# Experts' token rows: loaded from ScalarE's queue when the buffer is free, always as 112 partitions, and place 1 transposed two turns later

## The chip, the cores and the metric

The kernel runs on one core of one Trainium2 chip. The metric is the device time of one execution in microseconds, median of several runs.

## The reference

Four batches of 768 tokens go through a gated linear recurrence of eight heads (48 columns each), then through a mixture of eight experts of which each token takes one, then through a dense layer of 2048 hidden columns. All is float32.

```
state = alpha_t * state + k_t v_t        # per batch and head; y_t = q_t state
x = y as [3072, 384]
idx = argmax(x @ w_gate); g = softmax(x @ w_gate)[idx]
x = g * (relu(x @ w1[idx]) @ w2[idx])    # w1: 384 x 1024, w2: 1024 x 384
h = x @ w_in                             # 384 x 2048, comes as float64
out = (max(h, 0) + alpha2 * min(h, 0)) @ w_out
```

## The kernel before

The first 218 us or so are the recurrence (by chunks, as products) and the routing: each token's row goes by indirect DMA (`scatter`, L514, GpSimd's queue) to its expert's part of the table `xs` in DRAM, which has room for 448 rows (`CAP`) per expert. The six scatters of the last batch are still under way when the experts start.

The experts run in the order of their number of tokens, by places 0 to 7. `CAPS` gives the tokens that a place computes: 448, 448, 440, 424, 416, 400, 392, 384. A place has eight turns `f`; in a turn `expert_L1` makes 128 hidden columns of the first layer (9 products into `ph`), ScalarE writes their relu `hh`, VectorE the rest `hl`, and `expert_L2` adds the turn of two turns ago to the three sums `acc` (9 products). Each operand is the sum of two parts (`xh` and `xl`, `w1h` and `w1l`, `hh` and `hl`), so each product is three.

The rows of the next place are read by `expert_x` into the one buffer `xg`, in one DMA on SP's queue: as `CAPS[e] // 4` partitions of 4 rows, so 112, 110, 106, 104, 100, 98 and 96 partitions for the places 1 to 7. It is issued before the loop for place 1, and in turn 1 of the place before for the others. In turns 3, 4 and 5 `expert_xT` transposes 128 columns each into `pt` (TensorE), and `expert_xsplit` makes `xh` (ScalarE) and `xl` (VectorE) of them. `row_i` and `off_i` are tables with the place's first row in `xs` and its first place in the output; an engine that issues a DMA from there first reads them into a register (`value_load`). `expert_meta` copies the rows' gate weights and token numbers to `meta`.

Beside this, jobs on weights are handed out by turns (`job`, `one_job`). A `split` job loads a quarter of an expert's weights into `r1` and `r2` (SP's queue, three jobs ahead), copies them as `w1h` and `w2h` on ScalarE and subtracts on VectorE (`w1l`) and GpSimd (`w2l`). An `f64` job brings a piece of `w_in` or `w_out` from float64 to float32 by its bits: `fabs` on ScalarE (L166), four operations on VectorE (L169 to L173), and a store from SP's queue (L174). Place 0 has four f64 and four split jobs, places 1, 3 and 5 six and four, places 2 and 4 five and four, places 6 and 7 four split jobs alone.

The order of each engine's instructions is the order in which the code is written, and what a DMA has to wait for, the engine that issues it waits for. When the experts start, GpSimd clears the output table `yT` (L1201), which lies where the last rows were and so waits for the last scatter.

Of the kernel before, what the change touches and what calls it, by code (L numbers as in the profile page):

```python
# [20 lines left out]
P = 128  # L21
# [11 lines left out]
#: tokens that a place in the order of experts takes: the first expert, then the others, the fullest first  # L33
# [8 lines left out]
#: the upper word of 2**-126 as a float64, its bits read as a float32  # L42
# [4 lines left out]
class Kernel:  # L47
# [7 lines left out]
    # ------------------------------------------------------------ constants  # L55
# [11 lines left out]
    def constants(self, cp, ap):  # L67
# [11 lines left out]
        # per pair of heads: the 96 real columns of a padded 128, then the gate weights' rows  # L79
# [52 lines left out]
    # ------------------------------------------------------------ expert weights  # L132
    def w_src(self, e):
        """by place: the first expert, the others in their order, then the halves of the second layer"""
        if e == 0:
            return self.w1[0], self.w2[0]
        if e < E:
            if self.wreg[0] != e:
                self.wreg = e, self.nc.sync.value_load(self.perm_i[0:1, e:e + 1], min_val=0, max_val=E - 1)
            r = self.wreg[1]  # L140
            return (w[ds(r, 1)].rearrange("o a b -> (o a) b") for w in (self.w1, self.w2))
        h = e - E
        return self.w_in32[:, F * h:F * (h + 1)], self.w_out32[F * h:F * (h + 1), :]

    # w_in and w_out come as float64: here each is brought to float32, by its bits
# [14 lines left out]
    def f64_piece(self, n, raw, pool):  # L160
# [11 lines left out]
        # what float32 has no exponent for goes to zero  # L172
# [3 lines left out]
    # jobs on the weights, by their turns; what each reads is loaded some jobs ahead  # L176
# [68 lines left out]
    # ------------------------------------------------------------ attention  # L245
# [16 lines left out]
    def warm(self, n, cols=BLK):  # L262
        """products of no use while the first loads are under way: the array's clock comes up by them"""
        if n:
            ps = self.psg.tile([P, cols], F32, name="psw", tag="psG")
        for _ in range(n):
            self.nc.tensor.matmul(ps, self.wm, self.wm[:, 0:1].to_broadcast([P, cols]), start=True, stop=True)
# [51 lines left out]
    def attn_alpha(self, u, half, ps=None):  # L319
# [4 lines left out]
        # a decay outside the range is the recurrence's; here it only has to stay finite  # L324
        nc.vector.tensor_scalar(self.seq(self.sl[u % 2]["E"][:, 0:S], half), ps, ALO, AHI, ALU.max, ALU.min)

    def attn_scan(self, u, half=None):
        """decays from each step to its chunk's end and from the chunk's start, of all chunks or of half of them"""
# [101 lines left out]
    def attn_back(self, u, half):  # L430
# [12 lines left out]
        # the last logits are waited for, elsewhere the rows are  # L443
# [9 lines left out]
    # ------------------------------------------------------------ routing  # L453
    def route1(self, b, r, rp):
        """one-hot expert of a batch's tokens"""
# [18 lines left out]
    def route_gate(self, r, rp):  # L474
        """gate weight goes with the row"""
# [10 lines left out]
    def route2(self, b, rp):  # L486
        """slot of each token"""
# [24 lines left out]
    def scatter(self, dst, idx, src, n, group):  # L512
        """rows of src to rows of dst; those of a group go to rows that differ, so they need no order"""
# [13 lines left out]
    def totals(self, rp):  # L527
        """the experts' order, where each one's tokens start in it, and what lies beyond the capacities"""
# [42 lines left out]
    def attention(self, cp, rp, pp):  # L571
        nc, tc = self.nc, self.tc
        with ExitStack() as st:
            ap = st.enter_context(tc.tile_pool(name="attn", bufs=1))
            # what the unit before the last is done with makes room for the first expert's tokens
# [14 lines left out]
            # the first unit by halves, so that its products start early  # L590
# [126 lines left out]
    # ------------------------------------------------------------ the first expert's tokens  # L717
    # Those of the batches before the last come from xs. Those of the last batch are put in their columns by
    # products with one-hot rows, so that the first expert need not wait for their way through DRAM.
# [32 lines left out]
    def first_ranks(self, rp):  # L752
        """rank of the last batch's tokens in the first expert; far below 0 for those of others"""
# [19 lines left out]
    def ranks(self, ps, oh, before):  # L773
        """tokens of the same expert before each: in its tile, in the batch's tiles before it, before the batch"""
# [8 lines left out]
    # ------------------------------------------------------------ the experts  # L783
    def expert_rows(self, e):
        """rows of a place's expert"""
        r = 0 if e == 0 else self.nc.sync.value_load(self.row_i[0:1, e:e + 1], min_val=0, max_val=NSLOT - CAP)
        return self.xs[ds(r, CAPS[e]), :] if e else self.xs[0:CAPS[0], :]

    def expert_x(self, e):
        nc = self.nc  # L790
        rows = self.expert_rows(e)
        xg = self.op.tile([CAPS[e] // 4, 4, DM], F32, name="xg", tag="xg", bufs=1)
        nc.sync.dma_start(xg, rows[:, 0:DM].rearrange("(j p) w -> p j w", j=4))
        return xg, rows

    def expert_meta(self, e, rows):
        """gate weights and tokens go to their place in the experts' order"""
# [4 lines left out]
    def expert_xT(self, xg, x, m):  # L802
        nc = self.nc
        q = xg.shape[0]
        ps = self.pt.tile([P, 4 * q], F32, name="pt", tag="pt")
        for j in range(4):
            nc.tensor.transpose(ps[:, q * j:q * (j + 1)], xg[:, j, P * m:P * (m + 1)], self.ident[:q, :q])
# [10 lines left out]
    def mm3(self, ps, pairs, start, stop):  # L818
        """sum of products of operands that are each the sum of two parts"""
# [12 lines left out]
    def first_L1(self, w, f, x, n, first):  # L832
        """products of a turn of the first layer; of the first two turns, those with the last rows of x come last"""
# [41 lines left out]
    def experts(self):  # L875
# [15 lines left out]
        xgn, rows = self.expert_x(1)  # L891
        for e in range(E):
            for f in range(NF):
# [3 lines left out]
                if f == 1 and 0 < e < E - 1:  # L897
                    xgn, rows = self.expert_x(e + 1)
                if f >= 3 and f < 3 + NM and e + 1 < E:
                    if f == 3:  # L900
                        xn = self.expert_xset(e + 1)
                    self.expert_xT(xgn, xn, f - 3)
                self.job(self.gp, (e, f))
                if f == 5 and e == 0:
                    self.expert_meta(0, self.expert_rows(0))
                if f == 7 and e + 1 < E:
                    self.expert_meta(e + 1, rows)
            if e + 1 < E:
                x = xn
        # the last two turns by parts of the output, which the second layer takes up one after another  # L910
# [7 lines left out]
    # ------------------------------------------------------------ the second layer  # L918
# [39 lines left out]
    def ffn(self):  # L958
# [21 lines left out]
        # the last three turns, so that the tiles end one after another  # L980
# [3 lines left out]
    # ------------------------------------------------------------ what the fast path does not cover  # L984
# [9 lines left out]
    def recurrence(self, st):  # L994
        """For a decay outside [ALO, AHI]: the recurrence step by step, then the routing again."""
# [77 lines left out]
    def overflow(self):  # L1073
        """Tile after tile of tokens go through every expert and keep their own's; those beyond a capacity are put out."""
        nc, tc = self.nc, self.tc
        NF = F // P
        with tc.tile_pool(name="ovt", bufs=1) as sb:
            t = lambda n, s, d=F32: sb.tile(s, d, name=n, tag=n)
            # a token is put out where it is beyond its expert's capacity, or the fast path covers none
# [14 lines left out]
            # rows that no token was put in  # L1094
# [73 lines left out]
    # ------------------------------------------------------------ all of it  # L1168
    def run(self):
        nc, tc = self.nc, self.tc  # L1170
        with ExitStack() as st, tc.manual_schedule():
# [11 lines left out]
            # on the other side: the last rows are on their way to DRAM when the experts start  # L1183
# [57 lines left out]
```

## Time and profile before

| | |
|---|---|
| time, median of 3 runs | 906.2 us (901.11 to 907.78) |
| profiled execution, its span | 908.3 us; no other time of it is given |
| TensorE busy | 844.6 us, 93% |
| VectorE, ScalarE, GpSimd busy | 496.8, 304.9, 322.2 us |
| TensorE waiting for `xg`, 200 to 470 us | 33.3 us in 6 waits |
| moved by DMA | 90.53 MB, mean 100 GB/s |

Busy shares are means over stages that differ: the DMA engines are busy until about 470 us and nearly idle after that, while TensorE is busy to the end. So the rows to read are those of the experts' stage, about 218 to 490 us. The granted clock is TensorE's, as a share of 2.4 GHz; its other level is 0.5.

### The profile page before, as it was taken

What the parts mean: (1) busy time and instruction counts of PE and PEld (TensorE: products, weight loads), DVE (VectorE), ACT (ScalarE), POOL (GpSimd) and SP (SyncE); (2) the same over time, 40 slices, a digit from 0 to 9 for tenths busy, and PEclk for the clock granted to TensorE, in tenths of its full rate; (3) what the DMA queues carried; (4) which work ended last, traced back from release to release, by engine and by line L of the source; (5) the groups of instructions that cost most, each with busy time, mean ns of one, the idle gap of its engine ahead of it and who ended that gap; (6) DMA issues with size and microseconds to landing.
All of it is one profiled execution on the core that took longest, in us unless ns stands there. A gap on an engine that the chain in (4) does not pass through costs nothing. (4 is left out here: it accounts for less than half of the span.)

```text
span 908.3 us, 14260 instructions
## 1 busy us (share of the span) xinstructions
PE 844.6 (93%) x5330; PEld 745.1 (82%) x5330; DVE 496.8 (55%) x892; ACT 304.9 (34%) x596; POOL 322.2 (35%) x323
## 2 busy tenths in 40 slices
PE   7999999889899397798999999999999999999993
PEld 4777777659799297798899899999999999899993
DVE  8579797946978185677434543343343343343331
ACT  3455555542444153354344322122122112212111
POOL 6232525553622021122232724324334334325232
PEclk9799999978899698999999999999999999999997
DMA  9899898432685457659644000000000000000001
GB/s 145 169 255 196 177 159 175 93 102 85 200 246 165 144 139 229 211 171 265 192 118 106 19 1 18 18 1 25 11 1 33 3 1 35 1 1 35 1 1 39
DMA packets 153155, 90.53 MB, mean 100 GB/s; under 512 B 112716, under 2 KB 145780, under 8 KB 153076
## 3 DMA queue, kind: packets, MB, share of 16 engines
q1 hardware_dynamic: 148963, 74.45, 35.1%
q0 software_dynamic: 4112, 15.08, 4.6%
q8 instruction: 44, 0.72, 0.4%
q14 instruction: 36, 0.29, 0.1%
HBM read 68.14 MB, written 21.40 MB: 99 GB/s over the span
## 5 line engine op out<-in xcount | busy, mean ns | idle before, releaser
L941 POOL TENSOR_TENSOR gl<-g,gh 128x512 fp32r<-128x512 f32 x94 | 122.0, 1298 | 232.0 <-ACT gh L940 231.8
L938 DVE TENSOR_SCALAR g<-ph,al 128x512 f32<-128x512 f32 (+1 forms) x97 | 72.2, 744 | 225.0 <-PE ph L825 225.0
L823 PE MATMUL ph<-xh,w1h 128*128 128x512 f32 (+7 forms) x480 | 184.5, 384 | 0.0
L825 PE MATMUL ph<-xh,w1l 128*128 128x512 f32 (+7 forms) x480 | 184.5, 384 | 0.0
L824 PE MATMUL ph<-xl,w1h 128*128 128x512 f32 (+7 forms) x480 | 184.3, 384 | 0.0
L940 ACT CAST gh<-g 128x512 fp32r<-128x512 f32 (+1 forms) x97 | 59.7, 616 | 315.7 <-DVE g L939 297.8
L238 POOL TENSOR_TENSOR w2l<-r,w2h 128x768 fp32r<-128x768 f32 x38 | 74.9, 1973 | 206.2 <-ACT w2h L237 206.2
L825 PE MATMUL acc<-w2h,gl 128*128 128x384 f32 x384 | 130.0, 338 | 0.0
L823 PE MATMUL acc<-w2h,gh 128*128 128x384 f32 x384 | 129.3, 337 | 0.0
L824 PE MATMUL acc<-w2l,gh 128*128 128x384 f32 x384 | 129.0, 336 | 0.0
L825 PEld LDWEIGHTS ph<-xh,w1l 128*128 128x128 f32 x480 | 92.2, 192 | 12.8
L824 PEld LDWEIGHTS ph<-xl,w1h 128*128 128x128 f32 x480 | 92.3, 192 | 10.8 <-DVE xl L925 0.4
L823 PEld LDWEIGHTS ph<-xh,w1h 128*128 128x128 f32 x480 | 92.2, 192 | 9.9
L823 PEld LDWEIGHTS acc<-w2h,gh 128*128 128x128 f32 x384 | 72.2, 188 | 4.2
L824 PEld LDWEIGHTS acc<-w2l,gh 128*128 128x128 f32 x384 | 72.1, 188 | 4.1
L825 PEld LDWEIGHTS acc<-w2h,gl 128*128 128x128 f32 x384 | 72.0, 188 | 0.9 <-POOL gl L941 0.6
L823 PE MATMUL acc<-hh,w2h 128*128 128x448 f32 (+6 forms) x192 | 68.6, 358 | 0.0
L939 DVE SCALAR_TENSOR_TENSOR g<-ph,g 128x512 f32<-128x512 f32 (+1 forms) x97 | 66.5, 686 | 3.3
L824 PE MATMUL acc<-hl,w2h 128*128 128x448 f32 (+6 forms) x192 | 68.3, 356 | 0.0
L825 PE MATMUL acc<-hh,w2l 128*128 128x448 f32 (+6 forms) x192 | 68.1, 354 | 0.0
L380 POOL TENSOR_SCALAR_AFFINE_SELECT A<-A 128x384 f32<-128x384 f32 x64 | 38.5, 624 | 57.4 <-ACT A L379 57.4
L858 ACT ACTIVATE hh<-ph 128x448 fp32r<-128x448 f32 (+6 forms) x64 | 33.3, 520 | 76.0 <-PE ph L825 76.0
(178 smaller groups left out, 1230.9 us busy)
## 6 DMA issues: line engine op xcount, KB each, us to landing
r<-in_moe_w_dram SPq DMA_DIRECT2D x64, 384.0 KB
r<-in_moe_w_in_dram SPq DMA_DIRECT2D x16, 384.0 KB
r<-in_moe_w_out_dram SPq DMA_DIRECT2D x16, 384.0 KB
xs<-z POOLq DMA_DIRECT2D x7, 776.0 KB
k<-in_k_dram SPq DMA_DIRECT2D x32, 144.0 KB
q<-in_q_dram SPq DMA_DIRECT2D x32, 144.0 KB
v<-in_v_dram SPq DMA_DIRECT2D x32, 144.0 KB
a<-in_alpha_dram SPq DMA_DIRECT2D x30, 144.0 KB
```

Source lines behind the costliest of these rows:

```text
L238: (nc.gpsimd if r is r2 and not self.fast else nc.vector).tensor_tensor(l, r, h.bitcast(F32), ALU.subtract)
L380: nc.gpsimd.affine_select(out=a, in_=a, pattern=[[0, 3], [1, P]], compare_op=ALU.is_ge, fill=0.0, base=0, channel_multiplier=-1)
L823: mm(ps, ah, bh, start=start and i == 0, stop=False)
L824: mm(ps, ah, bl, start=False, stop=False)
L825: mm(ps, al, bh, start=False, stop=stop and i == n - 1)
L858: nc.scalar.activation(hh, ph, AF.Relu)
L938: nc.vector.tensor_scalar(g[:, cs], ph[:, cs], 0.0, self.al2[:, f:f + 1], ALU.min, ALU.mult)
L939: nc.vector.scalar_tensor_tensor(g[:, cs], ph[:, cs], 0.0, g[:, cs], ALU.max, ALU.add)
L940: nc.scalar.copy(gh[:, cs], g[:, cs])
L941: lo.tensor_tensor(gl[:, cs], g[:, cs], gh[:, cs].bitcast(F32), ALU.subtract)
```

## The change

Three things change in the experts' stage. `expert_x` reads 448 rows whatever the place computes, as 112 partitions of 4 rows, and `expert_xT` transposes three groups of 112 columns and one of what is left of `CAPS[e]`. The DMA and the register load for it are on ScalarE's queue, not SP's; for places 2 to 7 they come right behind the third transpose of the place before, which frees the buffer. The transposes stand in turns 4 to 6, and for place 1 (during place 0) in turns 5 to 7. `expert_meta` now reads its own row number on SP. The rest of the diff takes out comments.

```diff
-    def expert_rows(self, e):
-        r = 0 if e == 0 else self.nc.sync.value_load(self.row_i[0:1, e:e + 1], min_val=0, max_val=NSLOT - CAP)
-        return self.xs[ds(r, CAPS[e]), :] if e else self.xs[0:CAPS[0], :]
+    def expert_rows(self, e, n, eng):
+        r = 0 if e == 0 else eng.value_load(self.row_i[0:1, e:e + 1], min_val=0, max_val=NSLOT - CAP)
+        return self.xs[ds(r, n), :] if e else self.xs[0:n, :]
     def expert_x(self, e):
-        nc = self.nc
-        rows = self.expert_rows(e)
-        xg = self.op.tile([CAPS[e] // 4, 4, DM], F32, name="xg", tag="xg", bufs=1)
-        nc.sync.dma_start(xg, rows[:, 0:DM].rearrange("(j p) w -> p j w", j=4))
-        return xg, rows
-    def expert_meta(self, e, rows):
+        if e >= E:
+            return None
+        eng = self.nc.scalar
+        xg = self.op.tile([CAP // 4, 4, DM], F32, name="xg", tag="xg", bufs=1)
+        eng.dma_start(xg, self.expert_rows(e, CAP, eng)[:, 0:DM].rearrange("(j p) w -> p j w", j=4))
+        return xg
+    def expert_meta(self, e):
+        rows = self.expert_rows(e, CAPS[e], self.nc.sync)
...
-    def expert_xT(self, xg, x, m):
+    def expert_xT(self, e, xg, x, m):
         nc = self.nc
-        q = xg.shape[0]
-        ps = self.pt.tile([P, 4 * q], F32, name="pt", tag="pt")
+        n, q = CAPS[e], CAP // 4
+        ps = self.pt.tile([P, n], F32, name="pt", tag="pt")
         for j in range(4):
-            nc.tensor.transpose(ps[:, q * j:q * (j + 1)], xg[:, j, P * m:P * (m + 1)], self.ident[:q, :q])
+            k = min(q, n - q * j)
+            nc.tensor.transpose(ps[:, q * j:q * j + k], xg[:k, j, P * m:P * (m + 1)], self.ident[:k, :k])
...
-        xgn, rows = self.expert_x(1)
+        xg = self.expert_x(1)
         for e in range(E):
             for f in range(NF):
...
-                if f == 1 and 0 < e < E - 1:
-                    xgn, rows = self.expert_x(e + 1)
-                if f >= 3 and f < 3 + NM and e + 1 < E:
-                    if f == 3:
+                m = f - (5 if e == 0 else 4)
+                if 0 <= m < NM and e + 1 < E:
+                    if m == 0:
                         xn = self.expert_xset(e + 1)
-                    self.expert_xT(xgn, xn, f - 3)
+                    self.expert_xT(e + 1, xg, xn, m)
+                    if m == NM - 1:
+                        xg = self.expert_x(e + 2)
                 self.job(self.gp, (e, f))
                 if f == 5 and e == 0:
-                    self.expert_meta(0, self.expert_rows(0))
+                    self.expert_meta(0)
                 if f == 7 and e + 1 < E:
-                    self.expert_meta(e + 1, rows)
+                    self.expert_meta(e + 1)
```

The first place to see is ScalarE at the start of place 0. `px` are the first expert's columns, `r` the pieces of weights. Before:

```order
L812 CAST xh_83<-px 128x448 x3
L858 ACTIVATE hh<-ph 128x448
L166 ACTIVATE fabs<-r_2316 128x384
L858 ACTIVATE hh<-ph 128x448
L166 ACTIVATE fabs<-r_2473 128x384
```

Now, the same stretch:

```order
L817 CAST xh_83<-px 128x448 x3
L786 TENSOR_LOAD row_i
L786 ISA x2
L796 ISA
L796 DMA xg<-xs 112x4x384
L863 ACTIVATE hh<-ph 128x448
L166 ACTIVATE fabs<-r_2316 128x384
L863 ACTIVATE hh<-ph 128x448
```

The load of place 1's rows, with its wait for the last scatter, stands ahead of the first relu on ScalarE.

The second place is ScalarE later in place 0, from the third f64 job on. Before:

```order
L166 ACTIVATE fabs<-r_2592 128x384
L858 ACTIVATE hh<-ph 128x448
L812 CAST xh_2780<-pt 128x448
L237 CAST w1h_2821<-r_2847 128x3x256
L237 CAST w2h_2823<-r_2849 128x768
L858 ACTIVATE hh<-ph 128x448
L812 CAST xh_2780<-pt 128x448
```

Now, the same stretch, up to the first copy of transposed rows:

```order
L166 ACTIVATE fabs<-r_2592 128x384
L863 ACTIVATE hh<-ph 128x448
L237 CAST w1h_2821<-r_2847 128x3x256
L237 CAST w2h_2823<-r_2849 128x768
L863 ACTIVATE hh<-ph 128x448
L237 CAST w1h_2821<-r_2898 128x3x256
L237 CAST w2h_2823<-r_2900 128x768
L863 ACTIVATE hh<-ph 128x448
L817 CAST xh_2780<-pt 128x448
```

Place 1's first copy from `pt` stands two relus further down.

The third place is ScalarE in place 1, around the last transposes of place 2's rows. Before:

```order
L812 CAST xh_83<-pt 128x440
L237 CAST w1h_73<-r_3256 128x3x256
L237 CAST w2h_75<-r_3258 128x768
L858 ACTIVATE hh<-ph 128x448
L166 ACTIVATE fabs<-r_3298 128x384
```

Now, from the same copy on, which stands a turn later:

```order
L817 CAST xh_83<-pt 128x440
L786 TENSOR_LOAD row_i
L786 ISA x2
L796 ISA
L796 DMA xg<-xs 112x4x384
L166 ACTIVATE fabs<-r_3300 128x384
L863 ACTIVATE hh<-ph 128x448
```

The load of place 3's rows follows the third copy; before, it stood on SP's queue in turn 1 of place 2.

## Rows read from the trace of the kernel before

**Rows 1.** The cores: span and mean granted clock

```profile
core 0: 908.3 us, clock 0.956
```

**Rows 2.** Waits of TensorE, 200 to 470 us: total us, times, longest

```profile
PE pt L807 <- DMA xg<-xs: 33.3, 6, 15.2
```

**Rows 3.** Timeline of TensorE (start, us, [idle before]), first transposes of places 1, 3 to 7

```profile
233.06 1.01 PE L807 MATMUL pt<-ident,xg 112*128 112x112 f32 x4 [3.48 <-DMA xg<-xs]
...
312.06 0.94 PE L807 MATMUL pt<-ident,xg 106*128 106x106 f32 x4 [15.18 <-DMA xg<-xs]
...
349.04 0.93 PE L807 MATMUL pt<-ident,xg 104*128 104x104 f32 x4 [5.01 <-DMA xg<-xs]
...
385.00 0.54 PE L807 MATMUL pt<-ident,xg 100*128 100x100 f32 x4 [4.58 <-DMA xg<-xs]
...
417.57 0.53 PE L807 MATMUL pt<-ident,xg 98*128 98x98 f32 x4 [2.99 <-DMA xg<-xs]
...
446.69 0.72 PE L807 MATMUL pt<-ident,xg 96*128 96x96 f32 x4 [2.02 <-DMA xg<-xs]
```

**Rows 4.** Timeline of the SP queue: three loads of a place's rows

```profile
225.80 0.34 SPq L793 DMA_DIRECT2D xg<-xs  x1
...
291.81 0.30 SPq L793 DMA_DIRECT2D xg<-xs  x1
...
338.55 0.39 SPq L793 DMA_DIRECT2D xg<-xs  x1
```

**Rows 5.** Busy time by stretch: two waits, and place 1 (which has none)

```profile
core 0: us, PE busy (x) PEld busy (x) DVE busy (x) ACT busy (x) POOL busy (x), PEclk, DMA share, GB/s
297.00:302.00 5.00, 0.00 (x0) 0.00 (x0) 0.00 (x0) 0.00 (x0) 0.00 (x0) 0.81 0.13 50
344.00:349.00 5.00, 0.03 (x1) 0.00 (x0) 2.19 (x5) 0.63 (x2) 0.00 (x0) 0.89 1.08 283
254.00:291.00 37.00, 36.88 (x189) 33.86 (x188) 28.91 (x45) 19.10 (x36) 7.91 (x4) 1.00 0.74 209
```

**Rows 6.** The same view, stretches right behind the waits

```profile
233.00:239.00 6.00, 5.94 (x19) 5.41 (x20) 5.65 (x10) 3.04 (x6) 0.95 (x2) 0.53 0.34 98
312.00:325.00 13.00, 12.94 (x60) 12.04 (x61) 6.60 (x11) 6.05 (x11) 1.86 (x1) 0.80 0.36 115
349.00:360.00 11.00, 10.96 (x50) 10.47 (x51) 5.19 (x9) 4.04 (x8) 1.87 (x1) 0.74 0.61 216
385.00:397.00 12.00, 11.99 (x62) 11.73 (x63) 6.67 (x11) 6.25 (x12) 2.15 (x2) 0.86 0.55 189
417.50:430.00 12.50, 12.43 (x75) 12.38 (x76) 8.82 (x14) 6.72 (x12) 3.72 (x2) 1.00 0.85 294
447.00:460.00 13.00, 13.00 (x71) 12.93 (x70) 5.29 (x8) 5.76 (x10) 3.77 (x2) 0.87 0.35 113
```

**Rows 7.** Timeline of ScalarE, opening of place 0

```profile
221.77 0.55 ACT L858 ACTIVATE hh<-ph 128x448 fp32r<-128x448 f32 x1 [2.68 <-PE ph L825]
```

**Rows 8.** Timeline of GpSimd, same stretch

```profile
225.37 8.50 POOL L1201 MEMSET yT<- 128x10056 f32 x1 [2.29 <-DMA xs<-xb,slot]
```

**Rows 9.** Timeline of VectorE, same stretch

```profile
226.51 7.57 DVE L169 TENSOR_SCALAR ft<-r 128x384 uint32<-128x384 uint32 x1
234.12 0.56 DVE L170 SCALAR_TENSOR_TENSOR ft<-r,ft 128x384 uint32<-128x384 uint32 x1
```

**Rows 10.** Timeline of TensorE, second layer: first products of turns 0 and 2

```profile
223.96 0.37 PE L823 MATMUL acc<-hh,w2h 128*128 128x448 f32 x1
...
237.26 0.57 PE L823 MATMUL acc<-hh,w2h 128*128 128x448 f32 x1
```

**Rows 11.** Timeline of ScalarE, a product's relu behind a wait

```profile
235.96 0.56 ACT L166 ACTIVATE fabs<-r 128x384 f32<-128x384 f32 x1 [10.35 <-DVE ft L173]
236.43 0.52 ACT L858 ACTIVATE hh<-ph 128x448 fp32r<-128x448 f32 x1
```

**Rows 12.** Register load on ScalarE's queue: ns min/median/max

```profile
L871 ACTq TENSOR_LOAD <-off_i x7: 276/285/494, 287.9 to 485.9; - x7
```

## The prediction

> **What bounds the kernel now.** I read the clock line of the core first, then the waits of TensorE by releaser, then the timeline of each engine around each wait, and last the busy times by stretch. The program runs 908.3 us at a mean granted clock of 0.956 [rows 1], and TensorE carries the end. From 200 us on, where the experts run, it waits for one thing only: the rows of the next place in xg, six times, 33.3 us [rows 2]. The reader is to see that the six waits have different causes. Place 3's is the longest, 15.18 us [rows 3]; while it lasts the 16 DMA engines are 13% busy at 50 GB/s [rows 5]: a load in 106 partitions keeps only two engines busy. The waits of places 4 to 7 (5.01, 4.58, 2.99, 2.02 us) fall into stretches like 344 to 349, where the DMA engines are full (share 1.08, 283 GB/s): these loads are issued two turns ahead, and that is too late in a busy queue. From issue to first transpose place 3 takes 20.3 us and place 4 10.5 us [rows 3, 4]. Place 2 was loaded the same way and shows no wait. Place 1's wait (3.48 us) is in the opening, behind the last scatters; it is told apart below.
>
> Each wait costs twice. In the stretches right behind them TensorE is busy throughout, but at a granted clock of 0.80, 0.74, 0.86, 1.00 and 0.87 of 2.4 GHz [rows 6]: for some us the 1.2 GHz level is granted. Stretch times missing share gives the loss: 13 x 0.20 = 2.6, 11 x 0.26 = 2.9, 12 x 0.14 = 1.7, 0, 13 x 0.13 = 1.7, together **8.9 us**.
>
> **Part 1: loads one place ahead, all in 112 partitions.** A load now leaves right behind the third transpose of the rows before it (turn 6, in place 0 turn 7) and is needed in turn 4 of the next place, six turns later (five behind place 0). A turn is 18 products of two layers; place 1's stretch holds 189 products in 36.88 us [rows 5], so a turn is 3.5 us and the lead is 17 to 21 us. Apart from place 3, loads took 7.3 us (place 1) to 10.5 us (place 4) from issue to use [rows 3, 4]; the lead is some twice that. Place 3's 20.3 us would not be covered, but its cause goes with the 112 partitions: the only load of that form, place 1's, took 7.3 us in a stretch shared with other loads. So I take all five waits of places 3 to 7 away: 15.18 + 5.01 + 4.58 + 2.99 + 2.02 = **29.8 us**, and the 8.9 us of clock with them. The bounds: at least place 3's 15.18 + 2.6 = 17.8 us, at most all 38.7 us.
>
> The pages of the Trainium skill bear on both halves of this part. "DMA: Bandwidth & Descriptors" (section on why a DMA increments its semaphore by 16) says that a transfer runs on the largest count up to 16 that divides the slowest dimension of both sides; that is 2 for 106 partitions, and the trace agrees with 13% and 50 GB/s. The same page ("Issuing engines are not separate DMA queues") speaks against the other half: what ScalarE issues runs on the same 16 engines and saves only issue time. By that rule moving the loads to another queue gives nothing, and only the 17.8 us of place 3 are sure; its mechanism is the second rival below.
>
> What the part adds: seven times a register load (0.28 us [rows 12]) and an issue (0.30 to 0.39 us on SP [rows 4]) on ScalarE, under 1 us each. ScalarE is busy 19.10 of 37 us in place 1, so this hides. The loads stand behind the third xh copy, which has itself waited for the transposes; no new wait for the buffer. The extra rows (448 instead of 384 to 440) are at most 17% more bytes for a load. On SP the issue is replaced by nothing but a register load for the meta rows: a small gain, taken as zero. The transposes get the same columns in total (three of 112 and a rest): zero. In turn 6 the third part of x comes one turn nearer to its use, and at the end of place 0 directly before it: at worst a copy and a subtraction of 0.5 and 0.6 us that are not hidden; I count it in part 3.
>
> **Part 2: the opening of place 0.** Here the change adds a wait. The first load needs the last scatter of tokens, which lands at about 225.3: the memset of yT, released by the same scatter, starts at 225.37 [rows 8]. Before, SP stood in that wait and issued at 225.80 [rows 4]. Now ScalarE does, right behind the third xh copy and ahead of the first relu (221.77 before [rows 7]). That ScalarE doesn't pass a waiting instruction is seen at 235.96, where a relu for a product finished long before stands behind a waiting fabs [rows 11]. So:
> - The first relu starts at about 225.4 + 0.4 = 225.8, hl behind it ends near 227.0. TensorE, which began the second layer at 223.96 [rows 10], now waits till 227.0. It then has two half-turns ready (3.6 us, to 230.6).
> - On VectorE the first unsigned shift (L169) comes after hl, no longer before the memset. In the trace the one that met the memset (225.37 for 8.50 us) took 7.57 us, and ended at 234.1 as the memset did [rows 8, 9]. Now the first one is caught, and with it hl of turn 1 is behind it: 234.1 + three operations of some 0.6 + hl of 0.6 = 236.6. TensorE stands from 230.6 to 236.6.
> - Before, TensorE stood to 233.06 for xg, and its next second-layer turn came at 237.26 [rows 10], since hl of turn 2 was behind the same shift. So the old 3.48 us wait was mostly doubled by another and isn't won. At 236.6 the new order starts the second layer's turn 1, where the old one at 237.3 starts turn 2: one turn behind (3.65 us at full clock), less 0.7, plus two transposes that it still has to do more (under 0.6 us each by the repeat rows in [rows 3], 0.35 taken), is 3.6 us. The clock behind the wait was 0.53 for 6 us before (2.8 us lost [rows 6]); a later wait loses as much, later, of which about 2 us aren't matched before. Sum: **5.4 us lost**. Bounds: 2.5 (no clock loss that isn't matched, quick relu) to 7; and below zero if the shift isn't caught, which is the first rival.
>
> That GpSimd holds VectorE off for a whole instruction is what "SBUF — State Buffer" of the Trainium skill says (section "SBUF: two separate sides": one shared port pair, an exclusive lock); the 7.57 us row agrees, and by it a shift issued at 227 can't end before the memset.
>
> **Part 3: what is late next.** Without the waits, ten jobs on weights (loads, splits, float64 pieces) must fit into fewer us. Place 1 shows that they can: no wait, VectorE 28.91 and ScalarE 19.10 of 37 us busy, DMA share 0.74 [rows 5]. Place 5 has as many jobs in 400 columns instead of 448: VectorE 0.78 x 1.12 = 0.88 and DMA 0.83. Full, but not over. I take **3 us** of new waits, from 0 (place 1) to 10 (half of the waits of places 4 to 7 with half of their clock loss: 7.3 + 3.1).
>
> **Sum.** 908.3 - 29.8 - 8.9 + 5.4 + 3 = 878.0 us, that is 30.3 us less. The profiled execution spans 908.3 us, 0.5 us over the slowest of the timed runs (901.11, 906.2, 907.78): I see nothing outside the span, and set the 30.3 us against the median: **876 us**. By the bounds it is 906.2 - 38.7 + 2.5 = 870 to 906.2 - 38.7 + 7 + 10 = 884.5.
>
> **The rivals.**
> - The opening is won as well: if VectorE's shift isn't caught, or relu comes earlier, place 1's 3.48 us and its 2.8 us of clock are gained instead: 906.2 - 38.7 - 6.3 = 861, with half of that 864 to 868. For it: two turns more for the load. Against it: the 7.57 us row and the scatter's landing. Chance 0.10.
> - The transfers only collide elsewhere: DMA engines stay full at 283 GB/s where waits stand now, ScalarE waits for weights instead, and the waits of places 4 to 7 return (14.6 and 6.3 of clock, less the 3 counted): 876 + 18 = 894, half of it 885. For it: share 1.08 in those waits. Against it: place 1, and windows behind the waits that are not full. Chance 0.13.
> - Slower: ScalarE's strict order. Each load also waits for an older transfer's semaphore; if SP, which issues those, runs late, ScalarE stands with relu behind it. TensorE has two turns (7 us) of slack; to lose the 33.3 us of net gain (38.7 - 5.4) over six loads it must stand 5.6 us each beyond that, so ScalarE about 13 us at every load. From there it is 906 and more, at 15 us 918. In the trace ScalarE stood that long only once, 10.35 us [rows 11]. Chance 0.03.
> - The change doesn't do what it says: 112 partitions still go slowly, place 3's wait stays: 876 + 17.8 = 894, or nothing is won. Against: place 1's load. Chance 0.04.
>
> **How the numbers follow.** Forecast 0.70, rivals 0.10, 0.13, 0.03, 0.04. The range from 866 to 891 takes in the forecast with its bounds (870 to 884.5), the near half of the first rival and the smaller part of the second; it leaves out some 2 in 10. The three runs differ by 0.7%, so 1% is about what can be told from no change; that is 897 us. All of the forecast and the first rival and nearly all of the second lie below it: faster 0.93, same 0.04, slower 0.03.
>
> **What would show it.** TensorE's waits after 200 us no longer name xg; xg issues stand on ScalarE's queue seven times, each over 12 us ahead of its transposes; the granted clock is 1.0 from some 243 us until the end of the second layer. In the opening ScalarE waits for the scatter to 225.3, TensorE has two waits of about 3 and 6 us (for hh or hl of the first turns), and one shift on VectorE takes about 7 us. Wrong would be a wait of 3 us or more behind place 1 (part 3), or an opening that ends no later than before (part 2).

## The result, and the profile after

The changed kernel takes 871.62 us (median of 4 runs, 865.33 to 876.21), the kernel before 904.25 us (4 runs, 901.11 to 907.78). The ratio is 0.9651 with a 95% interval of 0.9591 to 0.9711: 3.5% faster. The forecast was 876 us against 906.2, a ratio of 0.967.

The cores' view of the changed kernel (span, mean granted clock), against [rows 1]:

```profile
core 0: 863.6 us, clock 0.985
```

The profiled spans differ by 44.7 us, 12 us more than the medians (32.6). Before any of it is explained, it has to be cut by stage. The next two rows are busy times by stretch, from the start of the program to the first product of the experts, in code that the change doesn't touch. Their columns are those of [rows 5]; the last but two is the granted clock. First the kernel before, with one stretch of it behind:

```profile
0.00:218.40 218.40, 203.18 (x2078) 153.64 (x2079) 164.53 (x410) 102.98 (x243) 93.52 (x165) 0.93 0.80 154
194.00:211.00 17.00, 15.50 (x84) 12.18 (x85) 10.04 (x26) 3.88 (x9) 5.05 (x4) 0.51 0.22 64
```

The same of the changed kernel:

```profile
0.00:203.71 203.71, 194.71 (x2079) 148.02 (x2079) 166.07 (x410) 102.82 (x243) 92.59 (x164) 0.98 0.88 165
```

The same 2,079 matmuls or so take 218.4 us at a clock of 0.93 in one execution and 203.7 us at 0.98 in the other; of the former, 17 us alone lie at 0.51, the lower level. In the kernels below this stage takes 203 to 219 us, whatever is changed behind it. So 14.7 of the 44.7 us lie ahead of it. The rest, 30.05 us, lies between the first product of the experts and the end: 908.34 - 218.40 = 689.94 us before, 863.60 - 203.71 = 659.89 after. The forecast's sum was 30.3. (The two parts are not wholly apart: the last scatter, seen by the memset that it releases, lands 7.0 us behind the first product of the experts before [rows 8] and 8.7 us behind it after, so some of what the faster start won is waited for in place 0. What that is worth is worked out in experiment 2.)

To place those 30 us I measure each place from the start of its first product of the first layer to that of the next place. In the timeline of TensorE of the changed kernel, place 0 and place 1 begin here, so that place 0 is 38.79 us long:

```profile
203.71 0.46 PE L828 MATMUL ph<-xh,w1h 128*128 128x448 f32 x1
...
242.50 0.45 PE L828 MATMUL ph<-xh,w1h 128*128 128x448 f32 x1
```

All lengths, worked out in the same way (us; "stage" is from the first product of place 0 to the end of the program):

| place | 0 | 1 | 2 | 3 | 4 | 5 | 6 | 7 | stage |
|---|---|---|---|---|---|---|---|---|---|
| before | 33.10 | 30.74 | 47.74 | 36.73 | 34.58 | 30.39 | 30.46 | 28.20 | 689.94 |
| after | 38.79 | 30.58 | 30.08 | 28.93 | 29.12 | 28.14 | 27.63 | 28.20 | 659.89 |
| difference | +5.69 | -0.16 | -17.66 | -7.80 | -5.46 | -2.25 | -2.83 | 0 | -30.05 |

Places 2 to 6 are those in which TensorE waited for the rows of places 3 to 7 [rows 3]. They give back 36.0 us; place 0 loses 5.7. The dense layer behind place 7 takes some 418 us in both (0.4 us more after).

The waits of TensorE from 200 to 470 us in the changed kernel, against [rows 2]: the 33.3 us for xg are gone, and the only two releasers left are both in place 0.

```profile
PE acc L829 <- DVE hl L864: 4.2, 2, 4.0
PE acc L828 <- ACT hh L863: 4.1, 1, 4.1
```

The load of place 2's rows now leaves on ScalarE's queue at 243.51 and meets its first transpose at 260.93, 17.4 us later (timeline); the page gives 4.8 us from issue to landing (DMA issues):

```profile
243.51 0.34 ACTq L796 DMA_DIRECT2D xg<-xs  x1
...
260.93 0.54 PE L812 MATMUL pt<-ident,xg 112*128 112x112 f32 x4
```

```profile
xg<-xs ACTq DMA_DIRECT2D x7, 672.0 KB, 4.8
```

Busy times by stretch, against [rows 5] and [rows 6]: a stretch in place 0, place 5, and everything from the end of the opening to the end of place 7.

```profile
223.50:227.50 4.00, 3.98 (x12) 3.57 (x13) 3.76 (x8) 2.39 (x4) 0.00 (x0) 0.57 0.78 257
361.20:389.30 28.10, 28.10 (x157) 27.37 (x157) 25.43 (x38) 15.31 (x29) 8.32 (x4) 1.00 0.83 247
227.50:445.00 217.50, 217.50 (x1179) 208.78 (x1178) 153.20 (x233) 112.28 (x198) 62.65 (x32) 1.00 0.72 218
```

From 227.5 us on TensorE is busy for all of 217.5 us at a granted clock of 1.00: no wait, and with it no half clock behind one. Place 5 has the DMA share of 0.83 that the prediction worked out, and VectorE at 25.43 of 28.10 us (0.90, forecast 0.88).

The opening of place 0, timeline of all engines, against [rows 7] to [rows 11]:

```profile
212.39 8.49 POOL L1208 MEMSET yT<- 128x10056 f32 x1 [3.74 <-DMA xs<-xb,slot]
212.46 0.40 ACTq L796 DMA_DIRECT2D xg<-xs  x1
212.91 0.54 ACT L863 ACTIVATE hh<-ph 128x448 fp32r<-128x448 f32 x1 [8.51 <-DMA r<-in_moe_w_dram]
...
213.50 0.51 PE L828 MATMUL acc<-hh,w2h 128*128 128x448 f32 x1 [4.07 <-ACT hh L863]
...
214.08 7.00 DVE L169 TENSOR_SCALAR ft<-r 128x384 uint32<-128x384 uint32 x1
...
222.85 0.62 DVE L864 SCALAR_TENSOR_TENSOR hl<-ph,hh 128x448 fp32r<-128x448 f32 x1
...
223.52 0.47 PE L829 MATMUL acc<-hl,w2h 128*128 128x448 f32 x1 [4.02 <-DVE hl L864]
```

Read it from the top. The last scatter lands at about 212.4 us and releases the memset on GpSimd and the first load on ScalarE's queue. The first relu starts only behind that load, at 212.91, after 8.51 us of idle time. (The profile names a load of weights as its releaser; the load of rows right ahead of it, and the memset with its releaser, say that it is the scatter.) TensorE gets its hh at 213.50, after 4.07 us. On VectorE the shift L169 begins under the memset and takes 7.00 us; hl of the next turn stands behind it until 222.85, and TensorE waits another 4.02 us.

### The profile page after: what moved, and what is told of

Read it like the earlier page. It is cut to its first block, busy times and chain, and to the rows that moved or that the text cites. A ratio compares the mean times of both kernels' runs of the same rounds, so it can differ in the third digit from the quotient of the medians.

```text
span 863.6 us, 14278 instructions
## 1 busy us (share of the span) xinstructions
PE 830.8 (96%) x5330; PEld 733.8 (85%) x5330; DVE 495.4 (57%) x892; ACT 306.8 (36%) x596; POOL 322.4 (37%) x323
## 5 line engine op out<-in xcount | busy, mean ns | idle before, releaser
L828 PE MATMUL ph<-xh,w1h 128*128 128x512 f32 (+7 forms) x480 | 181.8, 379 | 0.0
L830 PE MATMUL ph<-xh,w1l 128*128 128x512 f32 (+7 forms) x480 | 181.6, 378 | 0.0
L829 PE MATMUL ph<-xl,w1h 128*128 128x512 f32 (+7 forms) x480 | 181.6, 378 | 0.0
L830 PEld LDWEIGHTS ph<-xh,w1l 128*128 128x128 f32 x480 | 90.2, 188 | 12.6
L829 PEld LDWEIGHTS ph<-xl,w1h 128*128 128x128 f32 x480 | 90.3, 188 | 10.8 <-DVE xl L932 0.4
L238 DVE TENSOR_TENSOR w1l<-r,w1h 128x768 fp32r<-128x768 f32 x40 | 48.0, 1199 | 13.8 <-ACT w1h L237 13.1
```

Of the source, the lines that this page charges most:

```text
L238: (nc.gpsimd if r is r2 and not self.fast else nc.vector).tensor_tensor(l, r, h.bitcast(F32), ALU.subtract)
L828: mm(ps, ah, bh, start=start and i == 0, stop=False)
L829: mm(ps, ah, bl, start=False, stop=False)
L830: mm(ps, al, bh, start=False, stop=stop and i == n - 1)
```

## The experiments

In all of them a length of place is worked out as above, and a stage is from the first product of place 0 to the end, so that the clock of the part before the experts stays out of the comparison. Times are given with those of the kernel before on the same chip; kernels 1 and 8 have four runs, the others one, so the argument goes by the lengths in the profiled execution. Where an edit doesn't touch them, places 4 to 7 agree within 0.01 us from kernel to kernel (1, 2, 5, 6, 7 and the changed one); place 0 depends on when the last scatter lands.

**1. The first load alone back on SP.**

```diff
-        eng = self.nc.scalar
+        eng = self.nc.sync if e == 1 else self.nc.scalar
```

> Only place 1's load goes back to SP's queue; the other six stay on ScalarE. My theory (ScalarE's wait for the last scatter puts the first relu late, and with it the shift on VectorE under the memset): the first relu no longer waits, the first shift runs before the memset, the first wait of TensorE (4.1 us) goes; the second shift is caught instead, so one wait of 4 to 6 us stays. Place 0 takes 32 to 35 us instead of 38.8, the time is 4 to 7 us less than the changed kernel's, places 1 to 7 as there. Rival (the memset alone makes the opening, whoever issues the load): place 0 stays within 1.5 us of 38.8.

Place 0 is 34.42 us (4.4 less than after), the other places are as after; the stage is 655.62 us. The time is 873.19 us (868.35 to 876.38) against 910.74 before, a ratio of 0.957 (0.9519 to 0.9621); by itself it is not below the changed kernel's 871.62, as I had expected, but the kernel before takes longer here too. ScalarE's first relu no longer stands behind the scatter, TensorE's wait for hh is gone, and that for hl stays, as does the long shift (the waits of TensorE; then L169 on VectorE: ns min/median/max):

```profile
PE acc L829 <- DVE hl L864: 4.7, 1, 4.7
```

```profile
L169 DVE TENSOR_SCALAR ft<-r x32: 344/350/7477, 224.2 to 403.3; 128x384 uint32<-128x384 uint32 x32
```

So the in-order queue is one of two causes of the opening's loss, and the smaller one. The 4.4 us are too much for it: the scatter lands 6.9 us behind the first product here and 8.7 in the changed kernel; against kernels 3 and 5, with 7.0 and 6.9, place 0 is 3.5 to 3.7 us shorter.

**2. The memset of yT in 24 pieces.** The same zeros are written, by 24 instructions of 419 columns.

```diff
-                nc.gpsimd.memset(self.yT, 0.0)
+                for m in range(NM):
+                    for c in range(0, sum(CAPS), 419):
+                        nc.gpsimd.memset(self.yT[:, m, c:c + 419], 0.0)
```

> The changed kernel with the memset of yT in 24 pieces instead of one of 8.5 us. My theory: no shift is held longer than about one piece (under 1 us), the second wait of TensorE (4.0 us) goes and its first (4.1 us, for the scatter) stays; place 0 takes 34 to 36 us instead of 38.8. Rival (the 7 us of the shift are not the memset's hold, or GpSimd keeps VectorE off through all its pieces): the shift still takes about 7 us, place 0 stays near 38.8.

Place 0 is 31.35 us: 7.4 less than after, more than I had expected. The stage is 652.28 us, the time 867.99 (910.74 before). Beside the pieces no shift takes more than 0.65 us (7.00 under the one memset), and the wait for hl falls from 4.0 to 0.2; the wait for hh is ScalarE's stand for the scatter, which this kernel still has. It is 2.3 instead of 4.1 us because the scatter landed 6.9 us behind the first product in this execution, not 8.7; kernels 3 and 5, with 7.0 and 6.9 and waits of 2.4 and 2.3 us, show what that is worth (0.7 to 0.9 us of place 0), so some 6.6 of the 7.4 us are the memset's. (All shifts, those from 220 to 231 us, and the pieces:)

```profile
L169 DVE TENSOR_SCALAR ft<-r x32: 345/352/2017, 222.6 to 395.4; 128x384 uint32<-128x384 uint32 x32
L169 DVE TENSOR_SCALAR ft<-r x3: 515/633/649, 222.6 to 228.3; 128x384 uint32<-128x384 uint32 x3
L1210 POOL MEMSET yT<- x24: 444/447/661, 220.9 to 230.5; 128x419 f32 x24
```

The 2.02 us of the longest shift have nothing to do with the memset. That shift stands at 255.27, in place 1, beside a subtraction on GpSimd (timelines of GpSimd and VectorE); the changed kernel has one of 2.01 us at the same place.

```profile
255.18 1.90 POOL L238 TENSOR_TENSOR w2l<-r,w2h 128x768 fp32r<-128x768 f32 x1 [9.63 <-ACT w2h L237]
255.27 2.02 DVE L169 TENSOR_SCALAR ft<-r 128x384 uint32<-128x384 uint32 x1
```

The waits of TensorE:

```profile
PE acc L828 <- ACT hh L863: 2.3, 1, 2.3
PE acc L829 <- DVE hl L864: 0.2, 1, 0.2
```

**3. The old partitions, loaded early.** The change without its 112 partitions: each load again in a quarter of its own rows (106 partitions for place 3).

```diff
-        xg = self.op.tile([CAP // 4, 4, DM], F32, name="xg", tag="xg", bufs=1)
-        eng.dma_start(xg, self.expert_rows(e, CAP, eng)[:, 0:DM].rearrange("(j p) w -> p j w", j=4))
+        xg = self.op.tile([CAPS[e] // 4, 4, DM], F32, name="xg", tag="xg", bufs=1)
+        eng.dma_start(xg, self.expert_rows(e, CAPS[e], eng)[:, 0:DM].rearrange("(j p) w -> p j w", j=4))
...
-        n, q = CAPS[e], CAP // 4
+        n, q = CAPS[e], CAPS[e] // 4
```

> The changed kernel, but each load again in as many partitions as before (112, 110, 106, 104, 100, 98, 96); issued as early as in the change. My theory (the early issue wins all but the two-engine load, whose 14 us fit under a lead of 17 to 21 us): TensorE has no wait for xg of over 2 us; place 2, in which the load in 106 partitions was waited for, takes under 33 us (47.7 before, 30.1 in the change); perhaps weights behind it on the two engines are late by some us in place 1. Rival (112 partitions win place 2): place 2 or the one before it takes 35 us or more.

Places 0 to 7: 37.93, 30.57, 35.87, 28.87, 28.16, 27.31, 26.66, 28.21; the stage is 661.93 us, the time 880.45 (910.74 before). Place 2 is 5.8 us longer than after: here my theory missed (under 33), and the rival's bound (35 or more) was met. Two things are to be seen. The load in 106 partitions leaves at 282.69 and its first transpose starts at 305.87, 23.2 us later, more than the lead; and two loads of weights come late too, in two ways. One is issued behind it, at 293.36, and is there only at 305.06. The other SP issues only at 305.85: it stands 11.9 us, until the rows have landed. The timeline of ScalarE:

```profile
282.69 0.49 ACTq L796 DMA_DIRECT2D xg<-xs  x1
...
305.08 0.83 ACT L237 CAST w1h<-r 128x768 fp32r<-128x768 f32 x1 [6.40 <-DMA r<-in_moe_w_dram]
310.62 0.83 ACT L237 CAST w2h<-r 128x768 fp32r<-128x768 f32 x1 [4.71 <-DMA r<-in_moe_w_dram]
```

The timeline of SP with the two issues, then its wait ahead of the second (waits of SP, 285 to 312 us):

```profile
293.36 0.42 SPq L213 DMA_DIRECT2D r<-in_moe_w_dram  x1
...
305.85 0.38 SPq L215 DMA_DIRECT2D r<-in_moe_w_dram  x1
```

```profile
SPq L215 <- DMA xg<-xs: 11.9, 1, 11.9
```

The timeline of TensorE, first and second set of transposes:

```profile
305.87 0.55 PE L812 MATMUL pt<-ident,xg 106*128 106x106 f32 x4 [2.36 <-DMA xg<-xs]
...
313.10 0.58 PE L812 MATMUL pt<-ident,xg 106*128 106x106 f32 x4 [3.07 <-DVE xl L818]
```

And the busy times by stretch just ahead of the first of them, with DMA engines at 13% and 44 GB/s as in the wait of the kernel before [rows 5]:

```profile
300.00:305.00 5.00, 3.51 (x18) 2.95 (x16) 1.79 (x4) 0.00 (x0) 0.00 (x0) 1.00 0.13 44
```

A second thing was not expected at all: places 4 to 6 are 0.8 to 1.0 us *shorter* than in the changed kernel. Experiment 8 goes after that.

**4. Only the 112 partitions.** The kernel before, with loads from SP two turns ahead as it had them, but in 112 partitions.

```diff
-        return self.xs[ds(r, CAPS[e]), :] if e else self.xs[0:CAPS[0], :]
+        return self.xs[ds(r, CAP), :] if e else self.xs[0:CAPS[0], :]
...
-        xg = self.op.tile([CAPS[e] // 4, 4, DM], F32, name="xg", tag="xg", bufs=1)
+        xg = self.op.tile([CAP // 4, 4, DM], F32, name="xg", tag="xg", bufs=1)
...
-            nc.tensor.transpose(ps[:, q * j:q * (j + 1)], xg[:, j, P * m:P * (m + 1)], self.ident[:q, :q])
+            k = min(q, n - q * j)
+            nc.tensor.transpose(ps[:, q * j:q * j + k], xg[:k, j, P * m:P * (m + 1)], self.ident[:k, :k])
```

> The kernel before, with 112 partitions alone: loads on SP, in turn 1, transposes in turns 3 to 5. My theory: the long wait for place 3's rows falls from 15.2 us to 3 to 6 us, like its neighbours'; the waits of places 4 to 7 stay at 2 to 5 us each, as the issue is still late, with the clock loss behind them: places 2 to 6 together 160 to 172 us (179.9 before, 143.9 in the change). Rival (uneven loads make all the waits, 96 and 112 partitions being the only even ones): no wait for xg after place 1, places 2 to 6 together under 150 us.

Places 2 to 6: 35.14, 36.05, 35.55, 33.54, 30.85, together 171.1 us (before 179.9, after 143.9). The stage is 681.17 us, the time 900.17 (910.74 before). Place 2 wins 12.6 us, but places 4 and 5 lose 4.1, and TensorE still waits for xg six times:

```profile
PE pt L808 <- DMA xg<-xs: 21.3, 6, 4.6
```

Of the 4.1 us some 1.6 are the rests of 64 and 56 rows that experiment 8 is about. Partitions alone are worth 8.8 us in places 2 to 6, the earlier issue 27.2 us on top. In place 2 the two overlap: 112 partitions alone win 12.6 us there, early issue alone 11.9 (experiment 3), both 17.7.

**5. The transposes of place 1 back by two turns.**

```diff
-                m = f - (5 if e == 0 else 4)
+                m = f - (3 if e == 0 else 4)
```

> The changed kernel with place 1's transposes in turns 3 to 5 of place 0 again, the rest as in the change. My theory (in the changed opening the rows land long before turn 3, since TensorE stands for relu and for the shift): no wait for xg, place 0 within 1 us of 38.8. Rival (the two turns more are what keeps xg from being waited for): a wait for xg of 2 us or more, place 0 of 41 us or more.

Place 0 is 38.10 us, the stage 659.04 us, the time 874.3 (902.34 before); TensorE waits for hh (2.3 us) and hl (4.1), never for xg. Kernel 3, with the later turns and the same wait for hh, has 37.93 us: the turn makes no difference. In this opening the two turns bought nothing, because TensorE stands so long for hh and hl that the rows are there either way.

**6. Both causes of the opening taken away** (1 and 2 together), and **7. the same with the transposes of place 1 two turns earlier** (1, 2 and 5 together).

> The changed kernel with place 1's load on SP and the memset in 24 pieces. My theory (these two make the whole opening loss): no wait of TensorE of over 0.5 us in place 0, which takes 30 to 31 us (38.8 in the change, 34.4 and 31.4 with the one or the other alone); the experts' stage and what follows take 650.5 to 652 us. Rival (something else is in the opening, such as the weights' loads that follow on SP): 31.4 us or more.

> As the kernel with place 1's load on SP and the memset in pieces, but place 1's transposes in turns 3 to 5. My theory (with no other wait in the opening the rows are late for turn 3, and the two turns more earn something only here): a wait for xg of 2 to 4 us and the clock behind it, place 0 takes 33 to 36 us. Rival: the two turns earn nothing here either, place 0 stays within 0.7 us of the kernel with turns 5 to 7.

With both away, place 0 is 28.38 us, 10.4 less than after and 4.7 less than before, and 1.6 less than I had expected at best; the stage is 649.75 us (expected 650.5 to 652), the time 854.8 (902.34 before). One wait is left that counts, against my 0.5 us (TensorE):

```profile
PE acc L829 <- DVE hl L864: 1.4, 1, 1.4
```

With the transposes two turns earlier, place 0 is 36.38 us, 8.0 more, the stage 657.37, the time 865.65. Now TensorE does wait for the rows, and then for the copy of the transposed rows:

```profile
PE pt L812 <- DVE xl L818: 4.3, 1, 4.3
PE pt L812 <- DMA xg<-xs: 3.3, 1, 3.3
```

That is a little over the 36 us that I had expected at most, and the turn alone doesn't make all of it. The wait for the rows is the turn's. The copy `xl`, for which TensorE waits 4.3 us, stands on VectorE behind a shift, and this one was held among the pieces of the memset: it took 3.73 us and ended as the last piece did, at 225.0, where the same shift in kernel 6 took 0.85 (timeline of VectorE):

```profile
221.49 3.73 DVE L169 TENSOR_SCALAR ft<-r 128x384 uint32<-128x384 uint32 x1 [4.22 <-DMA w_in<-ft]
```

So the later transposes are worth 3.3 us at the least and 8.0 in this execution, but only where nothing else holds the opening. In the change itself that gain was hidden.

**8. All transposes of 112 columns** (kernel 6, with four full transposes in each set, whose surplus columns nobody reads).

```diff
-        ps = self.pt.tile([P, n], F32, name="pt", tag="pt")
+        ps = self.pt.tile([P, CAP], F32, name="pt", tag="pt")
...
-            k = min(q, n - q * j)
+            k = q
...
-        self.expert_xsplit(ps, x, m)
+        self.expert_xsplit(ps[:, 0:n], x, m)
```

> As the kernel with place 1's load on SP and the memset in pieces, and all four transposes of a set take 112 columns (the columns beyond the place's tokens are not read). My theory (a last transpose of 64, 56 or 48 rows costs more than one of 112): places 4 to 6, in which such rests stand, take 28.2, 27.4 and 26.8 us instead of 29.1, 28.1 and 27.6, the others stay within 0.1 us; the stage from the first expert on takes 648 to 650 us, the time is 10 to 13 us less than the changed kernel's. Rival (the places 4 to 6 lose their 0.9 us to something else, such as the loads): they stay within 0.2 us.

Places 4 to 6 are 28.28, 27.31 and 26.80 us, where the changed kernel has 29.12, 28.14 and 27.63: 2.5 us in three places, by transposing *more* columns. Here the busy times don't show the cost, the starts do. Groups of transposes of the changed kernel in place 4 (345 to 362 us), by form (busy time, mean ns of one):

```profile
L812 PE MATMUL pt<-ident,xg 112*128 112x112 f32 x9 | 1.4, 258 | 0.0
L812 PE MATMUL pt<-ident,xg 64*128 64x64 f32 x3 | 0.8, 272 | 0.0
```

A transpose of 64 rows is busy for 272 ns, one of 112 rows for 258: nearly the same. But the timeline of the changed kernel has a set of four with the product behind it, first with four of 112 rows, then with a rest of 80, then with a rest of 64:

```profile
234.10 0.55 PE L812 MATMUL pt<-ident,xg 112*128 112x112 f32 x4
234.42 0.45 PE L828 MATMUL ph<-xh,w1h 128*128 128x448 f32 x1
...
320.45 0.52 PE L812 MATMUL pt<-ident,xg 112*128 112x112 f32 x4
320.77 0.44 PE L828 MATMUL ph<-xh,w1h 128*128 128x424 f32 x1
...
349.02 0.66 PE L812 MATMUL pt<-ident,xg 112*128 112x112 f32 x4
349.60 0.45 PE L828 MATMUL ph<-xh,w1h 128*128 128x416 f32 x1
```

(The row names the form of the first of the four.) The set takes 0.32 us, 0.32 us, and with the rest of 64 rows 0.58 us. In this experiment the set at the same place is back to 0.32:

```profile
337.48 0.55 PE L812 MATMUL pt<-ident,xg 112*128 112x112 f32 x4
337.80 0.43 PE L828 MATMUL ph<-xh,w1h 128*128 128x416 f32 x1
```

Three sets in each of places 4 to 6 are 9 x 0.26 = 2.3 us; the sets with rests of 56 and 48 rows take 0.58 and 0.57. Start to start within the set, the rest of 64 comes 0.19 us after the third transpose instead of 0.095, and the product 0.20 after the rest instead of 0.03: it costs on both sides. The stage is 645.80 us, 14.1 less than that of the changed kernel, and the time 856.77 us (851.14 to 861.94) against 902.34 before, a ratio of 0.9497 (0.9424 to 0.9571). Only kernel 9 has a stage as short. I had expected 648 to 650 us and the other places within 0.1 us; against kernel 6 place 0 is another 0.94 us shorter (27.44; its wait for hl is 0.4 us, not 1.4) and place 3 0.43 (28.91).

**9. Kernel 8 with all loads on SP.**

```diff
-        eng = self.nc.sync if e == 1 else self.nc.scalar
+        eng = self.nc.sync
```

> As the kernel with place 1's load on SP, the memset in pieces and all transposes of 112 columns, but all seven loads on SP, at the same points of the program. My theory (what wins is that the load is issued a place ahead, not whose queue it is on; SP may stand in a wait for VectorE or GpSimd before it, but the lead is 17 to 21 us): no wait for xg of over 1 us, places 1 to 7 each within 0.3 us of the kernel with ScalarE's queue. Rival (SP's queue is what made the loads late): waits for xg in two or more places, 2 us or more each.

Places 0 to 7: 27.48, 30.55, 30.10, 28.91, 28.28, 27.31, 26.80, 28.20, each within 0.04 us of kernel 8; the stage is 645.98 us against 645.80. No wait for xg. The time, 866.22 (909.13 before, on another chip than kernel 8), is longer only in the part before the experts: 218.42 us, against 203.53. ScalarE's queue earns nothing; the early issue does, from either queue.

## Why the prediction was right, by its steps

**Waits and clock of places 2 to 6 (part 1).** Forecast 29.8 + 8.9 = 38.7 us, measured 36.0. Taken place by place, with each wait of [rows 3] and the loss worked out from [rows 6], the forecasts were 17.8, 7.9, 6.3, 3.0 and 3.7 us; measured were 17.66, 7.80, 5.46, 2.25 and 2.83. The first two fit within 0.2 us, the last three fall 0.7 to 0.9 us short each, for the reason under part 3. That a wait costs twice, by the time it takes and by the half clock behind it, is borne out by places 2 and 3: the waits alone would have been 15.2 and 5.0 us.

**What wins it.** The prediction gave two causes, the full-width load and the lead, and didn't split them. The runs do (3 and 4): where the load ran in 106 partitions either alone wins some 12 of 17.7 us, and in places 3 to 6 it is the lead alone (before 132.2 us together; partitions alone 136.0, of which the rests are some 2.3, lead alone 111.0). Its statement that 20.3 us "would not be covered" by a lead of 17 to 21 us was right: with the old partitions it took 23.2 us, and weights behind it were late as well, which the sum didn't have.

**ScalarE's queue.** The Trainium skill, "DMA: Bandwidth & Descriptors" (section "Issuing engines are not separate DMA queues"), was weighed against the change in the prediction. Experiment 9 agrees with the rule itself: SP and ScalarE give the same places within 0.04 us. What the prediction drew from it, that then only place 3's 17.8 us would be sure, doesn't follow: the lead comes from the place of the issue in the program, and that is free on either queue.

**The opening (part 2).** Forecast +5.4 us, measured +5.69, and by the steps named: the relu 0.45 us behind the load's issue, a first wait (forecast about 3 us, measured 4.1), a shift caught under the memset (7.00 us), a second wait (forecast 6, measured 4.0). The two waits sum to 8.1 us for a forecast of 9. Experiments 1 and 2 remove the causes one at a time (some 3.6 and 6.6 us at a like landing of the scatter), and 6 both (10.4 in all). The statement that the old wait of 3.48 us was mostly doubled by another is borne out by experiment 1: there nothing waits for xg, the scatter lands as before, and TensorE stands 4.7 us for hl instead. With both causes away the old wait is won: place 0 is 4.7 us shorter than before. Place 0 as a whole, before, after and in kernel 3 (busy times by stretch, columns as in [rows 5]):

```profile
218.40:251.50 33.10, 29.62 (x140) 26.88 (x140) 30.23 (x46) 13.57 (x24) 20.74 (x9) 0.90 0.62 193
```

```profile
203.71:242.50 38.79, 30.50 (x140) 27.04 (x140) 28.19 (x44) 12.70 (x22) 19.96 (x9) 0.91 0.57 182
```

```profile
216.76:254.69 37.93, 31.48 (x141) 27.87 (x140) 28.82 (x44) 12.72 (x22) 19.51 (x9) 0.87 0.59 186
```

The forecast had 3.6 us for the delay and about 2 for clock that isn't matched. In the changed kernel's execution TensorE's idle time is 4.8 us longer than before and its busy time, in which the clock shows, 0.9. But there the scatter landed 1.7 us later than before; in kernel 3, where it landed as before, the two are 3.0 and 1.9 us, so the parts have the forecast's size, the delay a little less. Kernels 3 and 5 lose 4.8 and 5.0 us in place 0. That the measured 5.69 comes within 0.3 us of the forecast owes something to the late landing, which is luck.

**What is late next (part 3).** This is the step that failed. Its 3 us of new waits are no waits at all: behind place 0 TensorE waits for nothing. A cost of nearly that size lies where the prediction said "the same columns in total (three of 112 and a rest): zero". Rests of 64, 56 and 48 rows cost 0.26 us a set, 2.3 us in places 4 to 6, and this is all but 0.4 of the 2.7 us missing in part 1. The sum came out at 30.05 for 30.3 because one term that wasn't there had nearly the size of what part 1 fell short by; that it came so near is luck.

**The rivals.** Transfers colliding elsewhere: DMA share 0.83 in place 5 and no wait, so it fell. ScalarE's strict order does cost, but at one load of seven, in the opening (some 3.6 us), where the sum had it. 112 partitions run at full width: place 2 is 30.08 us. The opening won as well: not by this change, but it was there to be won, as experiment 6 shows.

**The times.** The forecast set 30.3 us against the median of 906.2. By the medians it is 32.6; the stage says 30.05, and the difference is no more than the part before the experts varies by.

## What to carry to other kernels

Issue a load when its buffer comes free, on any queue that isn't an engine with urgent work behind it: the same load that cost nothing at six places cost some 3.6 us at the one where it had to wait for a scatter ahead of the relu that everybody needed. Before the gain of a change is explained, cut both traces at a point that the change can't touch; here 14.7 of 44.7 us lay ahead of it. And where a stall has several causes, one removed alone can show less than its worth (the later transposes: nothing, or 3.3 us and more), so take them away together before any is called useless.

## What the runs showed of the hardware that I had not expected

- Behind transposes of 112 rows one of 64, 56 or 48 rows costs more than one of 112, though its busy time is nearly the same (272 and 258 ns): a set of four takes 0.57 to 0.58 us instead of 0.32. Rests of 80, 88 and 104 rows don't show it. The Trainium skill, "TensorEngine Tiling (Array Packing)" (section "Key Properties"), says that a change of the tiling mode drains TensorE, and its section "Available Configurations" lists modes of 64 rows; the bound between 64 and 80 rows agrees with that, but that these transposes run in that mode is argued from it, not shown.
- A memset of 8.49 us on GpSimd held one VectorE instruction for 7.00 us; cut into 24 pieces of 0.45 us, which take 10 us together, the same shift took 0.52 to 0.65 us in experiment 2. Pieces are no safeguard, though: in experiment 7 a shift among them took 3.73 us, until the last piece had ended.
- A load in 106 partitions delays other loads (experiment 3): one that was issued behind it took 11.7 us to land, and SP stood 11.9 us for the rows before it issued another, with the DMA engines 13% busy from 300 to 305 us. ScalarE stood 6.40 and 4.71 us for the two.
